# Windowed attention and a low-rank mixer MLP on one core: q and k of eight head pairs transposed by SyncE's transfers, sums that clamp at zero, MLP sums one by one, a new order

## The chip, the cores and the metric

One core of one Trainium2 chip runs the whole program. The metric is device microseconds of one execution; three runs of the kernel before gave 224.15, 224.5 and 225.14 us (median 224.5). PE is TensorE, DVE is VectorE, ACT is ScalarE, POOL is GpSimd, SP is SyncE. [...]

## The reference

```python
# q, k, v: (4, 8, 768, 64); U: (768, 32); V: (32, 768); w_ch1: (512, 2048); w_ch2: (2048, 512); all float32
scores = scale * np.matmul(q, k.transpose(0, 1, 3, 2))
rel = pos[:, None] - pos[None, :]
is_global = pos[None, :] < 8
keep = is_global | ((rel >= 0) & (rel < 96))
dist = np.where(is_global & ~is_local, 96.0, np.abs(rel))
scores = np.where(keep, scores - slopes * dist, -1e9)
a = softmax(scores)
x = (a @ v).transpose(0, 2, 1, 3).reshape(4, 768, 512)
h = x.transpose(0, 2, 1) @ U @ V
u = x + h.transpose(0, 2, 1)
out = u + np.maximum(u @ w_ch1, 0.0) @ w_ch2
```

Of the 768 keys a query sees 8 global ones and the 96 last, so scores are made for a block of 128 queries against its own and the block before it, with the global keys written over 32 rows of the latter.

## The kernel before

**Order.** The kernel is a list of named tasks. Each is made by `add` with an engine, an expected duration, the tasks that it depends on, and the buffers that it takes (`acq`) and gives back (`rel`). `ORDER` names every task once. `Planner.run` goes through that list, gives each task a start by its engine's clock, its inputs and its buffers, and the program is then written in the order of these starts. Every engine works through its own tasks strictly in that order, so the relative order on one engine is the list's, and a task that waits holds up all behind it on its engine. A DMA counts as a task of the engine that issues it: POOL issues the loads (l..., w1_, w2_), SP the stores (O), copies of k and v (KO, VC, VG where CFG says S), and the first pair's loads.

**Attention.** The 4 batches have 8 heads each, two to a pair: pairs 0 to 15, four to a batch. For pair p, lk, lq and lv load k, q and v, cast to 16 bits, into staging buffers (three each for q and k). TK and TQ transpose them on PE by six matmuls with an identity (`flip`, line 608, matmul in line 611; pairs 1 to 3 by twelve of half width, `tr`, line 592) into one PSUM bank, and EK and EQ copy the result on DVE or ACT (`flat`, line 618, through `copy`, lines 362 and 364) into the tiles kT and qT, of which there are three each. KO makes kO, k moved by the global keys (line 653; by DMA through line 366). S makes the scores (line 734), with a bias matmul SB first in pairs 0 to 3; EX takes their exponential on ACT (line 799); MK multiplies by a mask on DVE in pairs 4 to 15 (lines 808, 812); PV multiplies by v and by vo (lines 866, 867); vo is v with the global rows, written by VC and VG. RC and NM divide by the sum (lines 901, 905), XC makes a 16-bit copy of x.

**Mixer.** UP transposes x on PE and multiplies it by U (lines 840, 845), XE and XU turn that small product, TE copies it, HM adds V's product (line 966) and E writes the sum u, transposed, into uT.

**MLP.** The first product has 16 blocks of 128 columns of w1 over 768 tokens. M1a and M1b are plain products (lines 1020, 1044); RL and RM clamp and evict them on ACT into htr (lines 1026, 1062). Pairs of blocks z and z + 8, for z of 4 to 7 in batches 1 and 2 and of 2 to 7 in batch 3, are made by Winograd's variant of Strassen's product: seven products (ZP1 to ZP7, line 1115) in place of eight. For that, ZT makes four sums of u, ZS four sums of w1's blocks (lines 1093 to 1096, kept over the batches for z of 4 to 7), and ZU, ZW, ZX, ZA, ZB, ZD, ZR evict and add the products (`ev`, lines 1133 and 1166). ZA, ZB and ZD are DVE sums of a PSUM bank and a stored product; since they don't clamp, ZQ and ZV clamp htr in place afterwards (lines 1172 and 1174).

The second product is made in the same way over all of w2: PA and PB make the sums of htr (lines 1199 to 1205; two instructions in each task, four pairs of tasks in a batch), TWa and TWb those of w2, RS starts the banks with the mixer's share (line 1238), P1 to P7 are the products (line 1246), DA to DH add them to x (lines 1258, 1285, 1298), O stores.

Where PE would wait in the early stages, the program puts matmuls of zeros (line 1347).

```python
            e1, e2 = ENG[CFG["ZQ"][z]], ENG[CFG["ZR"][z]]
            R1 = ev("Q", e1, ..., flat_relu(e1, htr[:, z]), [C11, C12], fast=1)
            R2 = ev("V", e2, ..., flat_relu(e2, quad(z + hj, 1)), [C22], fast=1)
            relus[z], relus[z + hj] = [R1, C11], [R2, C21]
```

Of the kernel before, what the change touches and what calls it, by code (L numbers as in the profile page):

```python
# [14 lines left out]
ALU = mybir.AluOpType  # L15
# [21 lines left out]
TWb1 S6.1 EX6.1 EX6.2 RS0.1 P10.1 P20.1 DA0.1 mask6 lv6 TQ8 P30.1 DF0.1 TK8 lq10 MK7.0 EQ8 UP5 XE5 VC7 P50.0 lq12
VG7 EK8 XU5 TE5 lk11 mask4 P30.0 DF0.0 S6.0 EX6.0 HM5 E05 MK6.2 P60.0 DB0.0 MK6.1 P60.1 DB0.1 S7.1 MK6.0 EX7.2 RS0.2
MK7.2 P10.2 DA0.2 P70.1 DD0.1 TQ10 lq11 EX7.1 MK7.1 TK9 EK9 KO9 ZS4 P70.0 lv11 TQ9 P20.2 EQ10 VC11 VC6 VG6 EQ9 TK10
EK10 KO10 DD0.0 P40.1 DG0.1 PV7 RC7 NM7 PV6 KO8 RC6 NM6 lv8 P60.2 P30.2 DC0.0 XC7 DB0.2 P50.1 DC0.1 XC6 UP7 UP6 XE7  # L40
DF0.2 P40.0 DG0.0 lv10 XE6 XU6 TE6 XU7 TE7 lv9 P70.2 DD0.2 HM6 E06 HM7 E07 S8.0 EX8.0 lq14 E17 ZP11.5 MK8.0 ZU1.5
# [5 lines left out]
O0.1 NM8 XC8 ZX1.7 PA1.1 S9.0 EX9.0 M1b1.5 M1b1.4 RM1.4 ZP51.6 ZB1.6 ZP41.6 RM1.5 UP8 XE8 MK9.0 ZP51.7 lk12 ZR1.6
TK12 EK12 TD1 ZP31.6 ZB1.7 M1a1.5 ZV1.7 ZD1.6 TQ12 RL1.5 XU8 EQ12 TE8 ZP41.7 ZR1.7 lv12 ZP31.7 ZD1.7 M1a1.0 M1b1.0
HM8 M1a1.1 M1b1.1 MK9.2 ZV1.6 RL1.0 ZQ1.6 ZQ1.7 PA1.3 PB1.1 E08 RL1.1 PA1.0 VG9 PV9 S10.1 RC9 RS1.1 P11.1 P21.1 lv14
P51.1 EX10.2 NM9 S10.0 PB1.3 PB1.0 DA1.1 EX10.1 XC9 S11.0 EX11.0 MK11.0 EX10.0 RS1.0 P21.0 P51.0 DC1.0 S11.1 EX11.2  # L50
P31.0 P11.0 MK10.1 P31.1 UP9 DF1.0 TQ14 VC12 EX11.1 DA1.0 P61.0 XE9 XU9 KO12 EQ14 TE9 MK11.2 MK11.1 VG11 PV11 lk14
TK14 lk15 EK14 DB1.0 P71.0 O1.0 DF1.1 P61.1 lq13 RC11 NM11 MK10.2 DD1.0 XC11 HM9 E09 S12.0 EX12.0 RS1.2 P11.2 P41.0
KO14 S12.1 EX12.1 DB1.1 P71.1 VG12 EX12.2 P31.2 DA1.2 MK10.0 VG10 DD1.1 PV10 MK12.0 TK13 EK13 P61.2 lq15 RC10 TQ13
EQ13 NM10 P21.2 XC10 KO13 UP10 lv13 UP11 XE10 DB1.2 P71.2 XU10 DF1.2 DC1.1 DG1.0 TE10 DD1.2 XE11 XU11 TE11 P41.1
DG1.1 VC14 O1.4 O1.3 HM10 E010 S14.0 EX14.0 HM11 E111 E011 MK12.1 MK14.0 P41.2 ZP12.7 ZU2.7 S14.1 EX14.2 ZT2 MK14.2
EX14.1 M1a2.5 ZP12.6 P51.2 DC1.2 M1a2.1 M1b2.1 TK15 EK15 KO15 ZU2.6 DG1.2 ZP62.6 RL2.5 ZP62.7 ZW2.6 M1b2.4 RL2.1
# [40 lines left out]
class Group:  # L97


    def __init__(self, kind, readers=1, n=1, among=None):  # L100
        self.kind, self.readers, self.n, self.among = kind, readers, n, among
        self.slot, self.since, self.free_at = None, None, 0.0
        self.read = self.written = 0.0


class Planner:


    LANES = 8

    def __init__(self, counts, dma_rate, switch):
        self.tasks, self.names = [], {}
        self.free = {k: [0.0] * n for k, n in counts.items()}
        self.held = []
        self.dma_rate, self.switch = dma_rate, switch

    def add(self, name, *a, **k):
        t = Task(name, *a, **k)
        if t.name in self.names:
            raise ValueError(name)  # L120
        self.names[name] = t
# [1277 lines left out]
```

## Time and profile before

| | |
|---|---|
| three runs | 224.15, 224.5, 225.14 us |
| profiled execution, span | 223.0 us |
| first matmul of the MLP | 28.1 us |
| last matmul starts | 219.5 us |
| matmuls of line 611, PE | 156 |
| filler matmuls (line 1347), busy | 4.2 us, 16 records |
| copies through PSUM into kT and qT by ACT, 768 wide | 17 of 0.81 us |
| granted TensorE clock | 1.000 |
| DMA: by POOL, by SP | 75.6% and 14.2% of 16 engines' span |

How to read it: the span reaches from the first to the last instruction of the profiled execution; the runs are timed around that. In the 40 slices one slice is 5.6 us. The busy time of PE counts the modelled end of each matmul, which overlaps the next one's start; the time from one start to the next is what a matmul takes of PE when it is packed. In a group's row, the first numbers after the bar are the busy time and the mean of one instruction in ns; after the second bar stands the idle time of the engine before the group, with what ended it. In the chain of waits each piece has its start, its length up to the next piece, and its engine and line. For a DMA, the time of the instruction is what SP or POOL needs to issue it, and the landing is counted from there.

### The profile page before, as it was taken

How to read it: one execution, taken by the hardware profiler on the slowest of the kernel's cores; microseconds unless marked ns; L12 is line 12 of the kernel's file. 1: busy time of each engine (PE TensorE's matmuls, PEld its weight loads, DVE VectorE, ACT ScalarE, POOL GpSimd, SP SyncE). 2: the span in 40 equal slices, each digit the busy share in tenths (PEclk: the TensorE clock that was granted, in tenths of full speed). 3: DMA queues.
4: the chain of work that ended last, by engine and by line, in shares of the span. 5: the costliest groups of instructions: out<-in, count | busy, mean ns of one | idle time of the engine just before them, and what ended most of it. 6: DMA issues, size and time to landing. Idle time of an engine off the chain costs nothing.

```text
span 223.0 us, 5965 instructions
## 1 busy us (share of the span) xinstructions
PE 216.4 (97%) x2424; PEld 158.5 (71%) x2424; DVE 181.6 (81%) x403; ACT 147.0 (66%) x260; POOL 73.7 (33%) x97
## 2 busy tenths in 40 slices
PE   8799899999999999999999999999999999999994
PEld 3466656675879976666888876666788875658883
DVE  5688966999987987888978688597978796889872
ACT  7888798768858669788757557787742458782000
POOL 8989959714894940010851000011000000000000
PEclk9999999999999999999999999999999999999999
DMA  6999999999999997662997021409100006000025
GB/s 173 178 170 149 159 161 185 184 206 166 158 157 92 140 191 141 224 46 37 68 116 98 18 79 65 132 4 71 33 0 3 0 3 259 25 1 3 0 97 190
DMA packets 87404, 23.31 MB, mean 104 GB/s; under 512 B 73840, under 2 KB 84784, under 8 KB 87376
## 3 DMA queue, kind: packets, MB, share of 16 engines
q0 software_dynamic: 72880, 13.74, 75.6%
q1 hardware_dynamic: 14496, 9.19, 14.2%
q8 instruction: 19, 0.31, 0.6%
q14 instruction: 9, 0.07, 0.1%
HBM read 27.56 MB, written 6.29 MB: 152 GB/s over the span
## 4 chain that ended last, share of the span: by engine, by line
PE 84%; DMA 7%; POOL 5%; issue 2%; DVE 1%; ACT 0%; DVEq 0%; POOLq 0%
PE ps L1246 34%; PE ps L1115 14%; PE ps L1020 11%; PE ps L1044 7%; PE ps L734 4%; DMA vt<-in_v_dram 4%; PE ps L611 3%; DMA stgq<-in_q_dram 3%; PE ps L840 2%; PE ps L867 2%; PE ps L866 2%; POOL stgq L457 1%; POOL w L507 1%; PE ps L1238 1%; PE ps L966 1%
## 5 line engine op out<-in xcount | busy, mean ns | idle before, releaser
L799 ACT ACTIVATE ep<-ps 128x1024 f16<-128x1024 f32 (+1 forms) x48 | 44.0, 952 | 16.3 <-PE ps L734 15.1
L1246 PEld LDWEIGHTS <-htr 128*128 128x128 f16 x392 | 36.2, 98 | 6.1 <-issue 1.9
L1020 PE MATMUL ps<-uT,w 128*128 128x384 f16 x176 | 33.3, 326 | 0.0
L1258 DVE TENSOR_TENSOR x_sb<-x_sb,ps 128x256 f32<-128x256 f32 (+1 forms) x60 | 26.8, 463 | 7.6 <-PE ps L1246 7.2
L1246 PEld LDWEIGHTS <-sA 128*128 128x128 f16 x288 | 27.4, 98 | 4.2 <-issue 0.7
L461 POOL DMA_DIRECT2D vt<-in_v_dram x16 | 16.7, 1047 | 32.9 <-PE ps L867 29.7
L1026 ACT ACTIVATE htr<-ps 128x384 f16<-128x384 f32 x44 | 20.7, 493 | 5.6 <-PE ps L1020 5.3
L1246 PE MATMUL ps<-w,sA 128*128 128x256 f16 x192 | 24.2, 273 | 0.0
L1246 PE MATMUL ps<-tB,htr 128*128 128x256 f16 (+1 forms) x200 | 24.2, 268 | 0.0
L1020 PEld LDWEIGHTS <-w 128*128 128x128 f16 x176 | 16.5, 98 | 10.6
L1246 PE MATMUL ps<-w,htr 128*128 128x256 f16 x192 | 23.5, 273 | 0.0
L457 POOL DMA_DIRECT2D stgq<-in_q_dram x24 | 19.9, 852 | 5.4 <-PE ps L611 3.3
L1044 PE MATMUL ps<-uT,w 128*128 128x384 f16 x112 | 21.3, 326 | 0.0
L457 POOL DMA_DIRECT2D stgk<-in_k_dram x24 | 20.0, 852 | 2.6 <-DMA w<-in_moe_w_ch_dram 1.0
L1133 DVE TENSOR_TENSOR htr<-ps,zu 128x384 f16<-128x384 f32 x30 | 16.4, 553 | 4.7 <-PE ps L1115 3.0
L362 ACT ACTIVATE zu<-ps 128x384 f32<-128x384 f32 x30 | 14.7, 493 | 5.7 <-PE ps L1115 5.3
L812 DVE TENSOR_TENSOR ep<-ep,mask 128x1024 f16<-128x1024 f16 x24 | 16.2, 684 | 1.4 <-ACT ep L799 0.9
L905 DVE TENSOR_TENSOR x_sb<-ps,rcp 128x768 f32<-128x768 f32 x16 | 15.3, 956 | 0.9 <-DMA vo<-vt 0.4
L1044 PEld LDWEIGHTS <-w 128*128 128x128 f16 x112 | 10.7, 98 | 6.6
L1115 PEld LDWEIGHTS <-w 128*128 128x128 f16 x108 | 10.2, 98 | 6.1
L734 PE MATMUL ps<-qT,kT 64*128 64x128 f16 x192 | 14.0, 217 | 0.4 <-DVE kT L364 0.4
L1115 PE MATMUL ps<-uT,w 128*128 128x384 f16 x56 | 13.4, 326 | 0.0
(124 smaller groups left out, 450.0 us busy)
## 6 DMA issues: line engine op xcount, KB each, us to landing
out_dram<-x_sb SPq DMA_DIRECT2D x20, 256.0 KB, 2.2
vt<-in_v_dram POOLq DMA_DIRECT2D x16, 192.0 KB, 5.9
stgk<-in_k_dram POOLq DMA_DIRECT2D x24, 96.0 KB, 6.6
stgq<-in_q_dram POOLq DMA_DIRECT2D x24, 96.0 KB, 5.6
w<-in_moe_w_ch_dram POOLq DMA_DIRECT2D x8, 256.0 KB, 7.1
w<-in_moe_w_ch_dram POOLq DMA_DIRECT2D x4, 512.0 KB, 11.7
vo<-vt SPq DMA_DIRECT2D x8, 123.8 KB, 2.5
out_dram<-x_sb SPq DMA_DIRECT2D x7, 128.0 KB, 2.2
```

Source lines behind the costliest of these rows:

```text
L457: nc.gpsimd.dma_start(o[:, i], src[b, h0 + i].rearrange("(n p) d -> p n d", p=P))
L461: nc.gpsimd.dma_start(vt[gv.slot][:, :, :, 0:D], v[b, h0:h0 + 2].rearrange("h (n p) d -> p h n d", p=P),)
L734: nc.tensor.matmul(t[:, hi, j * P:(j + 1) * P], lhs, qt[r, i * P:(i + 1) * P], start=not biased, stop=True, skip_group_check=biased,)
L799: nc.scalar.activation(ep[gep.slot][:, :, lo:512], ps[:, gsc.slot:gsc.slot + 2, lo:512], AF.Exp, scale=qk_scale)
L812: nc.vector.tensor_tensor(ev, ev, mv, ALU.mult)
L1020: nc.tensor.matmul(ps[:, g.slot, 0:HS], w1[:, dc, jt * P:(jt + 1) * P], ub[:, dc, i * HS:(i + 1) * HS], start=(dc == 0), stop=(dc == NDC - 1),
L1026: nc.scalar.activation(htr[:, jt, i * HS:(i + 1) * HS], ps[:, g.slot, 0:HS], AF.Relu)
L1044: nc.tensor.matmul(ps[:, g.slot + half, 0:HS], w1[:, dc, jt * P:(jt + 1) * P], ub[:, dc, half * HS:(half + 1) * HS], start=(dc == flat[0]) ...
L1115: nc.tensor.matmul(bank(g), a()[:, i], bq[:, i], start=first and i == 0, stop=last and i == 1, skip_group_check=True,)
L1133: return lambda: nc.vector.tensor_tensor(o, x(), y(), ALU.add)
L1246: nc.tensor.matmul(o if part is None else o[:, part], a[:, j, c0 + cols.start:c0 + cols.stop], bq[:, j] if part is None else bq[:, j, part ...
L1258: nc.vector.tensor_tensor(o, o, x, ALU.add)
```

## The change

What it does:

- For pairs 8 to 15 (`QD`), TK and TQ are gone, and EK and EQ are one transposing DMA each, issued by SP, from the staging buffer into kT or qT.
- ZA, ZB and ZD use one instruction that adds and clamps between 0 and 3e38; ZQ and ZV are gone.
- PA and PB are split into four tasks Sa, Sb, Sc, Sd of one instruction each. P5 now depends on the four Sa, P6 on Sb, P7 on Sc, P3 on Sd.
- The sums of w1's blocks are made for two blocks at a time (ZS1, ZS2, ZS3, 512 columns an instruction) and kept; batch 3's two extra blocks no longer use the buffers of the exponentials. The third set lies over the identity scaled for the bias and an early scratch tile, both of which have served by then.
- Some EK, EQ, KO, TE, XE, XC and E tasks move to another engine.
- The planner counts a small overlap of ACT's and DVE's instructions with the one before, and counts a transposing DMA as 1.0 of SP and 1.0 of transfer.
- `ORDER` is new throughout.
- Options that were not used are deleted, and one (`XD`, empty) is added.

```diff
-    "ZK": (4, 5, 6, 7), ... "ZR": "DDADDAAD", "ZQ": "DDAADDDD", "TE": "DAADAAAADADADAAD", "XE": "DAAAAAADAAAAAAAD",
-    "EK": "ADADDDADAADAAAAD", "EQ": "DDADAADDADADAAAA", "KO": "ADDDDDSDASASSAAD",
-    "XC": "DDDDDQAADADAAAQA", "E": "AAAAAADAADDAAAAA",
+    "ZK": (2, 3, 1),
+    "TE": "ADADAAAAADAAAAAA",
+    "XE": "AAADADAADAAAAAAA",
+    "EK": "ADDDDADDAADAAAAD",
+    "EQ": "DDDADDDDADADAAAA",
+    "KO": "ADDDDDDDASDSDDAS",
+    "XC": "DDDDDQAAADDAAAQD",
+    "E": "AAAAAADAAAAAADAA",
+    "TSP": 1.0,
+    "TSZ": 1.0,
+    "XD": (),
+    "NZS": 2,
+    "QD": (8, 9, 10, 11, 12, 13, 14, 15),
...
+    OVER = {ACT: 0.105, DVE: 0.08}
...
         def arrange(x, stg, gs, ld, gt, dst, i):
+            if p in CFG["QD"]:
+                def turn():
+                    o = dst().rearrange("c (n p) -> c n p", n=NB)
+                    nc.sync.dma_start_transpose(o, stg[gs.slot].rearrange("p a b -> p (a b)"))
+
+                return [add(SP, TSP, turn, ld, acq=[gt], rel=[gs], size=TSZ, name=f"E{x}{p}")]
             g = Group("ps", among=A1)
...
+                def sums_s(home=home, A11=A11, A12=A12, A21=A21, A22=A22):
+                    op = nc.vector.tensor_tensor
+                    op(home[:, 1], A11, A21, ALU.subtract)
+                    op(A21, A21, A22, ALU.add)
+                    op(home[:, 0], A21, A11, ALU.subtract)
+                    op(home[:, 2], A12, home[:, 0], ALU.subtract)
...
             def tt(o, x, y):
-                return lambda: nc.vector.tensor_tensor(o, x(), y(), ALU.add)
+                return lambda: nc.vector._custom_dve(TENSOR_ADD_SAT, out=o, in0=x(), in1=y(), s0=3.0e38, s1=0.0)
...
-            R1 = ev("Q", e1, {ACT: 0.84, DVE: 0.4, POOL: 2.2}[e1], flat_relu(e1, htr[:, z]), [C11, C12], fast=1)
-            R2 = ev("V", e2, {ACT: 0.47, DVE: 0.26, POOL: 1.16}[e2], flat_relu(e2, quad(z + hj, 1)), [C22], fast=1)
-            relus[z], relus[z + hj] = [R1, C11], [R2, C21]
+            relus[z], relus[z + hj] = [C11, C12], [C22, C21]
...
-            p1 = add(ea, 0.57 if by_dma else 1.14, pre1, need, fast=2 if by_dma else 12, name=f"PA{b}.{g}")
-            p2 = add(eb, 1.02 if eb == DVE else 4.6, pre2, [p1] + war(3), fast=12, name=f"PB{b}.{g}")
-            pa += [p1, p2]
+            def one(nm, o, x, y, op, dp):
+                return add(DVE, 0.555, lambda: nc.vector.tensor_tensor(o, x, y, op), dp, fast=2, name=f"{nm}{b}.{g}")
+
+            T1 = one("Sa", s1, a21, a22, ALU.add, need + war(5))
+            T3 = one("Sc", a21, a11, a21, ALU.subtract, [T1])
+            T2 = one("Sb", s2, s1, a11, ALU.subtract, [T1] + war(6))
+            T4 = one("Sd", s4, a12, s2, ALU.subtract, [T2] + war(3))
```

The parts of the two lists that the prediction speaks of; first around the start of the MLP, before and after:

```diff
-VG3 EX2.0 E00 SB3.2 w1_7 S3.2 w1_6 PV2 RC2 NM2 UP1 XC2 EX3.0 TQ4 EX3.2 lk7 PV3.0 PV3.1 PV3.2 RC3.2 XE1 XU1 RC3.0
-M1a0.3 M1c0.3 HM3 E03 vs2 E13 KO5 S4.1 lv4 EX4.1 mask0 EX4.2 M1d0.3 M1b0.3 RL0.3 M1a0.14 M1b0.14 w1_4 RL0.14 M1b0.15
-lq6 M1b0.13 RM0.13 M1a0.2 M1c0.2 TK7 M1d0.2 MK4.1 RM0.15 w1_2 MK4.2 VC4 M1a0.13 VG4 RM0.14 EK7 KO7 RL0.13 M1b0.2
+TK5 XU2 E01 TE2 UP3.0 UP3.1 HM2 EK5 UP3.2 EQ4 S4.0 NM3 XE3 E02 XU3 TE3 KO5 S4.1 HM3 EX4.0 w1_0 E03 E13 M1a0.1 lq5
+M1c0.1 w1_3 M1d0.1 M1b0.1 lk6 w1_2 mixl TK6 EX4.1 RL0.1 M1b0.6 EX4.2 M1a0.5 TQ5 M1b0.7 M1a0.6 RL0.5 RM0.6 mask0 EK6
+EQ5 KO6 TD0 RM0.7 S5.1 MK4.2 RL0.6 MK4.0 lk7 w1_5 vs2 lv4 EX5.2 MK5.2 VC4 lv5 w1_7 S5.0 EX5.0 M1a0.11 M1b0.4 lq6 EX5.1
```

and in the new list around the last transposing DMAs:

```diff
+DC1.1 lq13 lv12 VC12 DD1.1 DD1.2 lv14 lk13 UP11 XE11 EQ14 P41.2 XE10 XU11 XU10 DF1.0 TE11 DB1.0 P71.0 DG1.2 VG12 TE10
+S14.0 HM11 HM10 E111 E010 DD1.0 E011 ZT2 P41.1 EX14.0 ZP12.6 P41.0 ZP22.6 M1a2.0 ZP12.7 ZU2.6 M1b2.0 ZP62.6 DG1.1
...
+ZU2.5 ZB2.6 ZP12.4 ZP22.5 ZP62.7 ZW2.7 M1a2.6 ZA2.5 MK12.1 ZP42.6 ZP32.6 ZP62.5 ZA2.7 O1.5 EK15 VG15 VC15 VC14 O1.2
+O1.3 O1.1 EQ13 ZU2.4 EQ15 M1b2.6 ZP22.4 RL2.6 ZW2.5 ZD2.6 ZP72.7 ZR2.6 ZA2.4 RM2.6 ZX2.7 ZP62.4 ZW2.4 S14.1 ZP52.7
...
+MK14.0 O1.4 MK14.2 Sa2.3 MK14.1 PV12 ZP52.5 KO15 RM2.4 ZP42.5 RC12 ZR2.4 NM12 PV14 RL2.2 ZR2.5 S13.0 EX13.0 RC14 ZB2.5
```

More of the change, by code (lines that the diff above doesn't have):

```diff
@@ L37 @@
[L37 to L41, printed above, removed]
@@ L47 @@
[L47 to L51, printed above, removed]
@@ L52 @@
[L52 to L56, printed above, removed]
@@ new lines @@
+lv8 lq10 M1b0.13 M1b0.11 TWa1 TWb1 PV6 M1a0.14 RM0.13 UP5 M1a0.13 RL0.14 RM0.11 RC6 NM6 Sa0.1 RL0.15 XE5 RL0.13
+M1b0.14 S7.0 RS0.2 XU5 P10.2 VG7 VC7 VC8 RM0.14 RS0.0 VG8 EQ8 EK9 EK8 EQ9 KO9 Sa0.2 Sb0.2 Sc0.2 EX7.0 Sb0.1 MK7.2
+DA0.2 TWa0 RS0.1 lv10 TE5 lk12 Sa0.3 Sb0.3 HM5 Sd0.2 Sd0.3 MK7.1 P20.0 lv9 P20.1 lq11 lk15 E05 P10.0 XC6 UP6 P50.1
+P10.1 Sd0.1 XE6 XU6 TE6 Sc0.3 TWb0 P50.2 HM6 E06 DA0.1 DA0.0 P30.1 P20.2 P30.0 MK7.0 Sc0.1 P60.1 P60.2 DC0.1 DB0.1 PV7
+RC7 P60.0 P50.0 NM7 P70.1 DF0.0 DC0.0 XC7 UP7 XE7 DB0.2 DB0.0 DD0.1 DF0.1 P30.2 DF0.2 XU7 P70.0 TE7 HM7 E17 E07 DD0.0
@@ L186, in run @@
             s = max(r, clock[t.eng])
+            if t.eng in self.OVER and t.eng in last:
+                p = last[t.eng]
+                s = max(r, p.start + 0.02, clock[t.eng] + (0.035 if p in t.deps else -self.OVER[t.eng]))
+                if p in t.deps:
+                    s = max(s, p.end + 0.035)
+            last[t.eng] = t
             if t.eng == PE and t.mode != mode:
@@ L342 @@
     zu = sb("zu", [P, HS], FP32, CFG["NZU"])
-    zs = sb("zs", [P, len(ZK), 3, 2, P], FP16) if ZK else None
+    NZS = CFG["NZS"]
+    zs = sb("zs", [P, NZS, 3, 2, 2 * P], FP16)
+    zh = [zs[:, i] for i in range(NZS)] + [ibe[:, 0:12 * P].rearrange("p (i a c) -> p i a c", i=3, a=2)]
     assert hj == H and HS == 384
@@ L934, in attention @@
             XC = add(
-                xe, 0.9 if xq else {DVE: 0.55, POOL: 0.88, ACT: 0.84}[xe], cast, [NM], acq=[gx16], size=1.2 if xq else 0.0, fast=1, name=f"XC{p}",
+                xe, 0.9 if xq else {DVE: 0.6, POOL: 0.88, ACT: 0.84}[xe], cast, [NM], acq=[gx16], size=1.2 if xq else 0.0, fast=1, name=f"XC{p}",
             )
+            gx16.readers = 1 + turned
             UP = add(
-                PE, 0.49 if xu else 0.67, mixed(range(NB)), [XC, c_u16], lat=0.3, acq=[gx], rel=[gx16],
+                PE, 0.16 if turned else 0.49, mixed(range(NB)), [XC, c_u16], lat=0.3, acq=[gx], rel=[gx16],
@@ new lines, in attention, with xturn, xuevac @@
+            if turned:
+                def xturn():
+                    o = uT[b % 2][:, hp].rearrange("p (n c) -> p n c", n=NB)
+                    nc.sync.dma_start_transpose(o, x16[gx16.slot].rearrange("p n c -> p (n c)"))
+                XT = [
+                    add(
+                        SP, TSP, xturn, [XC] + (mm1_done[b - 2] if b >= 2 else []), size=TSZ, rel=[gx16], name=f"XT{p}",
+                    )
+                ]
+        gxu = Group("xu")
+        def xuevac():
+            copy(ENG[CFG["XE"][p]], xus[gxu.slot], ps[:, gx.slot, 384:384 + R].unsqueeze(1).broadcast_to((P, RG, R)))
@@ L956, in tevac, with xuturn @@
+        def xuturn():
+            nc.tensor.matmul(
+                ps[:, gx.slot + 1, 384:512], xus[gxu.slot].rearrange("p g r -> p (g r)"), ident16,
+                start=turned, stop=True, skip_group_check=True,
+            )
+        XE = add(ENG[CFG["XE"][p]], 0.28, xuevac, [UP], acq=[gxu], name=f"XE{p}")
+        UP = add(PE, 0.06, xuturn, [XE], lat=0.3, rel=[gxu], name=f"XU{p}")
+        if split:
+            assert not turned
+            XT = []
         def tevac():
-            copy(ENG[CFG["TE"][p]], tmp[b % 2][:, hp * P:(hp + 1) * P], ps[:, gx.slot + int(xu), 384:512])
+            copy(ENG[CFG["TE"][p]], tmp[b % 2][:, hp * P:(hp + 1) * P], ps[:, gx.slot + 1, 384:512])
@@ L1110, in bank, with pr @@
                 return ps[:, g.slot, 0:HS]
-            def pr(n, g, a, bq, dp, reads=False, first=False, last=False, z=z, gs=gs):
+            def pr(n, g, a, bq, dp, reads=False, first=False, last=False, z=z):
                 def go():
@@ L1119, in pr @@
                 t = add(
-                    PE, 0.327, go, dp, lat=0.3, acq=[g] if first else [], bw=[] if first else [g],
-                    rel=[gs] if reads and gs else [], name=f"ZP{n}{b}.{z}",
+                    PE, 0.327, go, dp, lat=0.3, acq=[g] if first else [], bw=[] if first else [g], name=f"ZP{n}{b}.{z}",
                 )
@@ L1300, in mlp @@
             DC = add(DVE, 0.7, both, [P5], rel=[gX], name=f"DC{b}.{t}")
-            if acc:
-                def onto(gst=gst, t=t):
-                    nc.gpsimd.dma_start(xb[:, t + ht], late[gst.slot], accum_op=ALU.add)
-                DG = add(POOL, 1.0, onto, [DD, DG, DC], rel=[gst], size=0.9, name=f"AX{b}.{t}")
             def store(tt, c0, c1):
```

292 lines of the change are left out of this document (126 added, 166 removed).

## The prediction

> **What bounds the kernel now.** I read the page first (busy shares, then the 40 slices), then the chain of waits in order of time, then the groups by line, then the SP queue's own issues.
>
> ```profile
> span 223.0 us, 5965 instructions
> ...
> PE 216.4 (97%) x2424; PEld 158.5 (71%) x2424; DVE 181.6 (81%) x403; ACT 147.0 (66%) x260; POOL 73.7 (33%) x97
> ...
> PE   8799899999999999999999999999999999999994
> ```
>
> PE is the bound, and from the eighth slice (39 us) to the last but one it has no hole. A busy PE can still hide waits, because a matmul's end is modelled: the groups give 0.22 us for one transpose, while starts lie much closer. So the price of PE work is taken from the chain, where a piece lasts until the next one starts:
>
> ```profile
> 60.02 0.34 PE ps L611 x6
> 60.36 0.87 PE ps L1246 x8
> 61.23 0.33 PE ps L611 x6
> ```
>
> Six transposes of one q or k hold PE for 0.34 us, 0.057 us each, with no pause before or behind. The transposes are thus on the path, at that price. Before 39 us the chain is another one: loads, and engines that wait for them.
>
> ```profile
> 26.86 8.09 DMA vt<-in_v_dram
> ...
> 34.97 0.77 DVE vo L364
> ...
> 36.01 0.55 DVE kT L364
> ...
> 36.60 0.34 PE ps L734 x6
> ```
>
> Here the copy of v for pair 4 (VC4) stood at the head of DVE's queue until its load landed at 34.95; the k of a later pair was written behind it, and PE's scores started at 36.60.
>
> **The change part by part.**
>
> *Transposes off PE.* For pairs 8 to 15, TK and TQ go: 16 tasks of 6 matmuls, 16 x 0.34 = 5.4 us of PE, all of it after 58 us, where PE is packed. Nothing replaces it on PE. This is the main term: -5.4. Adding up the PE tasks of the two order lists at prices from such rows gives 204.7 before and 199.3 after, so no other PE work changes. Stretches of row-grouped matmuls (scores, mixing, rest) between full ones are 35 before and 38 after by my count in the lists; a change of kind costs PE some 0.1 us (an estimate: sixteen scores hold 0.55 us, but the six of 36.60 hold 0.34 with the change behind them). I take +0.3, bounds 0 to 0.6.
>
> *Their evictions.* Sixteen PSUM copies go too: 12 on ACT (0.81 each, 9.7 us) and 4 on DVE (0.56, 2.2 us). Worth nothing on the path: neither engine ends a wait of PE there (the only compute engine that PE itself is seen waiting for after the first microseconds is DVE, 0.4 us, at 36.6).
>
> *The transfers that replace them.* SP gets 16 issues that the trace of before doesn't show. The nearest rows are SP's other SBUF-to-SBUF transfers:
>
> ```profile
> L366 SPq DMA_DIRECT2D vo<-vt x24: 585/616/2116, 62.1 to 156.5; - x24
> ...
> L366 SPq DMA_DIRECT2D kO<-kT x8: 612/650/1747, 46.2 to 102.7; - x8
> ...
> DMA to landing us min/median/max: 1.9/2.4/9.2
> ```
>
> Between 0.6 and 2.1 us to issue, 1.9 to 9.2 us to landing for 120 KB; these move 192 KB. I take 1.0 us of SP and 4 us to landing (kO's median is 3.9), since size and kind are kO's. That is 16 us of SP over 90 us, in a queue with holes of up to 27 us. Does any come too late? By PE work counted along the new list, EK8, EQ8, EK9 and EQ9 stand 17 us ahead of the first score that reads them (S9.0), EK10 and EQ10 7 us (S10.1), EK14 17 us, but EQ14 only 2.0 us before S14.0 and EK13 2.2 us before S13.0. A place in the list is no time: SP runs ahead where it is free. Ahead of EK13, SP holds EK15, the copies of v for 15 and 14, four stores, EQ13 and EQ15; the first can start when the second MLP's sums end, 19 us of PE work before S13.0. Four transfers at t, nine plain issues at about 0.5 and 4 us to landing and copy: 4t + 8.5, so 12.5 at t = 1.0, and no wait below t = 2.6. EQ14 waits for its load (lq14, 16 us of PE work ahead; loads land in 3.6 to 14.5) and then 4 us. I charge +0.4 for small waits at S14.0 and S13.0; bounds 0 (landing in time) and 4 (2 us at each). Behind a transfer that waits on SP stand stores and copies of v; PV waits for the copies, and a store's buffer is next written two batches on, which is far.
>
> [...]
>
> *Sums that clamp.* 42 sums (ZA, ZB, ZD) clamp at zero, and ZQ and ZV go.
>
> ```profile
> L1133 DVE TENSOR_TENSOR htr<-ps,zu 128x384 f16<-128x384 f32 x30 | 16.4, 553 | 4.7 <-PE ps L1115 3.0
> ...
> L1174 DVE TENSOR_SCALAR htr<-htr 128x768 f16<-128x768 f16 x12 | 4.1, 355 | 0.2
> ...
> 183.00:201.30 18.30, 18.30 (x123) 11.06 (x121) 15.00 (x34) 14.71 (x33) 0.00 (x0) 1.00 0.23 87
> ```
>
> Gone: 12 x 0.355 and 7 x 0.255 = 6.0 us of DVE, 5.2 us of ACT. The new sum isn't in the trace; same operands and count as the old, so I take 0.55; it can hardly be below the 0.355 of a clamp alone, and 1.1 (a second pass) is the other end. At 0.55 the path gains nothing, since PE covers it. The cover is thinnest in the last MLP's first product, 183 to 201.3: DVE 15.0 of 18.3, of which its 18 sums are 9.9. It loses 2.2 in clamps there; at 1.1 the sums add 9.9, 22.7 in 18.3: 4.4 us late.
>
> *The rest.* Weight sums: 24 instructions of 0.28 become 12 of about 0.42 (between 0.28 for 256 columns and 0.55 for 768), -1.7 us of DVE. PA and PB become four tasks each of the same instructions: 64 x 0.55, unchanged, free to lie apart. Moves between engines (EK and EQ of pairs 0 to 7, KO, TE, XC, E) add about 2.6 us to DVE. DVE ends near 174 of 181.6, ACT near 129 of 147. All of it lies under PE.
>
> *New order, start.* Until its first MLP matmul at 28.1 us, PE has 4.2 us of filler matmuls and some waits, one of 0.5 at 36.60 shown above. In the new list VC4 comes after the first scores of pair 5, and lv4 after the loads of k for pairs 5 to 7, so that block goes: -0.5. Other loads move by one or two places of about 0.85 us on POOL; bounds -3 (most filler gone) to +2.
>
> Sum: 223.0 - 5.4 + 0.3 + 0.4 - 0.5 = 217.8 us of span. The runs' median is 224.5, 1.5 over the profiled span, so **219.3 us**.
>
> **The rivals.**
> - *The start gains more.* Speaks for it: ACT and DVE are both near 80% busy before 30 us, and six evictions there change engines. Against: real PE work ahead of the first MLP matmul is the same 17 to 18 us in both lists, and the loads' time isn't changed. 3 us more: 216.3.
> - *Waits at S14.0 and S13.0 take much of it.* Loads of 14 land late and each score waits 2 us: 219.3 + 3.6 = 222.9, with no difference if another microsecond follows.
> - *Slower: the transposes fill SP.* If one holds SP or its rings for t, the stretch EK15 to EK13 is 4t + 8.5 against 19 us. Waits begin at t = 2.6, the gain is gone at t = 4.0, and t = 5.3 gives 219.3 + 4 x 2.7 = 230; at the 9.2 us of the longest landing, 245. For it: kO's landing varies fourfold. Against: no SP issue in the trace passes 2.1 us.
> - *The clamped sum costs 1.1:* the last stage comes 4.4 us late, 223.7; no change.
>
> **How the numbers follow.** The forecast 0.61, own range 217 to 221.5; better start 0.15; waits at two scores 0.09; costly sum 0.04; slower 0.11. A measurement of this kernel can't tell 0.5% (1.1 us) from no change. Faster (under 223.4): 0.61 + 0.15 + most of the waits = 0.84; same 0.05; slower 0.11. The range 215 to 224.5 leaves out the slower case and a small part below.
>
> **What would show it.** Right: no L611 rows of pairs 8 to 15, PE's matmuls fewer by 96, PE without holes from 40 us, SP's transposes under 2.6 us each, L1174 and L1172 gone with the sums still near 0.55. Wrong: PE idle at scores of pairs 8 to 15 with a DMA into qT or kT as releaser; sums near 1 us; a first MLP matmul later than 30 us.

## Result and the profile after

| | before | after |
|---|---|---|
| median of four runs beside each other | 224.56 us | 232.29 us (230.72 to 232.99) |
| ratio, 95% interval | | 1.0333 [1.0292, 1.0374] |
| span of the profiled execution | 223.0 us | 231.2 us |
| mean granted TensorE clock | 1.000 | 0.976 |

The kernel became 3.3% slower; the forecast was 219.3 us. Some executions of a kernel take over 1.5% longer than its fastest, and all times and ratios here leave those out. Every ratio below is against the kernel before, run beside it (medians 224.5 to 225.1 us). The page of the kernel after, its head and the 40 slices (one slice is 5.8 us):

```profile
span 231.2 us, 5730 instructions
...
PE 216.4 (94%) x2330; PEld 154.9 (67%) x2330; DVE 172.9 (75%) x374; ACT 129.1 (56%) x235; POOL 74.0 (32%) x97
...
PE   8999997999999389999976999999999999999994
...
PEclk9999999999999959999997999999999999999999
DMA  7999999999994993999499957851300001000346
```

PE now has two holes, in slices 14 and 15 (75 to 87 us) and in slices 21 and 22 (116 to 127 us), and at each the clock digit falls, to 5 and to 7. The last row is one that the prediction didn't read: no slice of the DMA engines is under 0.9 from 6 to some 70 us. In the kernel before this stretch reaches to 84 us:

```profile
DMA  6999999999999997662997021409100006000025
```

The row adds up the times of all packets and is cut off at 9. The times of packets that overlap count together, so the share of a window can pass 1 (2.30 from 80 to 85 us, below); a stretch of 0.9 or more is called full here.

To see where time goes I price all PE work at its packed start-to-start times from the trace: 205.2 us before, 199.9 us after. At a moment, that moment plus the work still to do is the earliest end still open. Where a column grows from one row to the next, that time was lost (e1, e2, e3 and e6 are experiments, described below):

| at | before | after | e1 | e2 | e3 | e6 |
|---|---|---|---|---|---|---|
| 28 us | 214.4 | 207.6 | 208.0 | 207.8 | 208.1 | 207.3 |
| 75 us | 216.2 | 211.5 | 210.8 | 211.6 | 211.4 | 211.6 |
| 90 us | 216.7 | 219.5 | 212.8 | 217.2 | 213.8 | 212.7 |
| 110 us | 217.1 | 220.0 | 213.6 | 217.9 | 214.7 | 213.7 |
| 130 us | 217.8 | 226.0 | 219.4 | 220.2 | 216.4 | 214.4 |
| last matmul | 219.5 | 227.8 | 221.1 | 222.0 | 218.1 | 216.0 |

At 75 us the kernel after is 4.7 us ahead. It loses 8.0 us between 75 and 90 and 6.0 between 110 and 130 (before: 0.5 and 0.7). The chain of waits of the kernel after shows the first hole (start, length, engine and line; L652 is the transposing transfer, L408 SP's copies, L767 the scores, L1263 the second product):

```profile
75.97 0.56 SPq L652
...
76.63 0.69 SPq L408
...
77.38 4.28 DMA kO<-kT
...
81.79 0.40 PE ps L767 x4
82.19 5.17 PE ps L1263 x24
```

S9.0 waits for q of pair 9, and then for kO9, the last thing that SP issued. The 24 matmuls behind take 5.17 us; at the packed 0.109 us they are 2.6. Why SP is late stands in its own timeline of the kernel after (start, us, instruction):

```profile
68.26 1.91 SPq L408 DMA_DIRECT2D vo<-vt  x3
70.28 2.08 SPq L652 DMA_TRANSPOSE qT<-stgq  x1
72.55 2.61 SPq L652 DMA_TRANSPOSE kT<-stgk  x2
75.32 1.21 SPq L652 DMA_TRANSPOSE qT<-stgq  x1
76.63 1.39 SPq L408 DMA_DIRECT2D kO<-kT  x2
```

and in SP's waits of that stretch:

```profile
SPq L408 <- DMA vt<-in_v_dram: 19.6, 1, 19.6
```

VC8, the copy of v for pair 8, stands ahead of EQ8 in SP's list and waited until v8 had landed at 68.2. The four transfers and KO9 came in one row behind it. The second hole, by the chain (L832 is the exponential, L404 ACT's copy that makes KO14):

```profile
116.38 5.21 DMA kT<-stgk
...
121.62 0.83 ACT kO L404 x2
122.45 0.92 ACT ep L832
...
125.79 3.01 PE ps L1263 x16
```

EK14 was issued at 116.4 and landed at 121.6. KO14 waited for it on ACT, in front of the exponential of pair 11, for which PV11 waited on PE. And SP came late to EK14 because KO11, also on SP, had waited for the landing of EK11:

```profile
SPq L408 <- DMA kT<-stgk: 5.1, 1, 5.1
```

The clock of both holes, by windows of the kernel after (PE, PEld, DVE, ACT and POOL busy, then the granted clock, DMA share, GB/s):

```profile
75.00:80.00 5.00, 2.12 (x20) 1.42 (x17) 2.44 (x6) 0.90 (x3) 4.16 (x5) 1.00 1.18 140
80.00:85.00 5.00, 3.21 (x18) 2.23 (x19) 0.69 (x1) 1.53 (x3) 3.42 (x5) 0.53 2.30 151
85.00:90.00 5.00, 5.00 (x49) 3.48 (x48) 1.65 (x5) 2.32 (x3) 0.00 (x0) 0.78 0.29 21
90.00:95.00 5.00, 5.00 (x45) 2.99 (x43) 4.86 (x11) 4.37 (x7) 0.00 (x0) 1.00 0.87 265
```

So of the 8.0 us some 5 are the waits themselves and 2.6 the slower clock behind them. The 0.53 and 0.78 are means of windows of 5 us: in shorter windows the trace has 0.50 from 80.3 to 87.2 us and 1.00 around it, and behind the second hole 0.50 from 124.7 to 128.1 us.

The transfers and the clamped sums themselves, by line of the kernel after (issue time in ns min/median/max):

```profile
L652 SPq DMA_TRANSPOSE qT<-stgq x8: 1210/1253/2085, 70.3 to 148.0; - x8
L652 SPq DMA_TRANSPOSE kT<-stgk x8: 1212/1245/2033, 72.6 to 150.7; - x8
...
  POOL stgk L499: 22.8, 3
...
DMA to landing us min/median/max: 2.7/3.6/6.4
```

```profile
L1182 DVE CUSTOM_DVE_ANT_0 htr<-ps,zu 128x384 f16<-128x384 f32 x30 | 16.3, 553 | 12.4 <-PE ps L1165 7.9
```

At the median a transfer costs SP 1.25 us and lands 3.6 us after its issue, both near the 1.0 and 4 of the forecast (EK11 and EK14, of the second hole, took 6.4 and 5.2), and the clamped sum takes the 553 ns of the plain one. POOL waited 22.8 us in all for k's staging buffers to be given back.

### The profile page after: what moved, and what is told of

It reads as the page before. It is cut to its first block, busy times and chain, and to the rows that moved or that the text cites. A ratio compares the mean times of both kernels' runs of the same rounds, so it can differ in the third digit from the quotient of the medians.

```text
span 231.2 us, 5730 instructions
## 1 busy us (share of the span) xinstructions
PE 216.4 (94%) x2330; PEld 154.9 (67%) x2330; DVE 172.9 (75%) x374; ACT 129.1 (56%) x235; POOL 74.0 (32%) x97
## 4 chain that ended last, share of the span: by engine, by line
PE 78%; DMA 10%; DVE 4%; POOL 3%; ACT 2%; issue 1%; SPq 1%; DVEq 0%; ACTq 0%; POOLq 0%
PE ps L1263 31%; PE ps L1165 14%; PE ps L1071 8%; PE ps L1095 7%; PE ps L767 4%; DMA stgq<-in_q_dram 4%; PE ps L895 2%; DMA kT<-stgk 2%; DMA x<-x_sb 2%; PE ps L874 2%; PE ps L748 2%; DMA kO<-kT 2%; PE ps L894 2%; PE ps L1255 1%; PE ps L1350 1%; PE ps L1009 1%
## 5 line engine op out<-in xcount | busy, mean ns | idle before, releaser
L832 ACT ACTIVATE ep<-ps 128x1024 f16<-128x1024 f32 (+1 forms) x48 | 44.3, 953 | 16.9 <-PE ps L767 16.4
L1263 PEld LDWEIGHTS <-htr 128*128 128x128 f16 x392 | 37.7, 101 | 7.4 <-issue 2.1
L1071 PE MATMUL ps<-uT,w 128*128 128x384 f16 x176 | 33.9, 326 | 0.1
L1263 PEld LDWEIGHTS <-sA 128*128 128x128 f16 x288 | 27.8, 100 | 4.6 <-issue 0.8
L499 POOL DMA_DIRECT2D stgk<-in_k_dram x24 | 19.9, 844 | 24.3 <-DMA kT<-stgk 22.8
L1263 PE MATMUL ps<-tB,htr 128*128 128x256 f16 (+1 forms) x200 | 26.0, 286 | 0.0
L1182 DVE CUSTOM_DVE_ANT_0 htr<-ps,zu 128x384 f16<-128x384 f32 x30 | 16.3, 553 | 12.4 <-PE ps L1165 7.9
L1263 PE MATMUL ps<-w,sA 128*128 128x256 f16 x192 | 24.7, 274 | 0.0
L1077 ACT ACTIVATE htr<-ps 128x384 f16<-128x384 f32 x44 | 20.6, 493 | 6.4 <-PE ps L1071 6.2
L1263 PE MATMUL ps<-w,htr 128*128 128x256 f16 x192 | 23.8, 273 | 0.0
L1071 PEld LDWEIGHTS <-w 128*128 128x128 f16 x176 | 16.2, 98 | 10.5 <-DMA w<-in_moe_w_ch_dram 0.5
L1095 PE MATMUL ps<-uT,w 128*128 128x384 f16 x112 | 21.3, 326 | 0.0
L404 ACT ACTIVATE zu<-ps 128x384 f32<-128x384 f32 x30 | 14.2, 495 | 6.9 <-PE ps L1165 6.6
L767 PE MATMUL ps<-qT,kT 64*128 64x128 f16 x192 | 14.6, 220 | 2.0 <-DMA qT<-stgq 2.0
L895 PE MATMUL ps<-vt,ep 128*128 128x65 f16 x192 | 13.3, 193 | 3.2 <-ACT ep L832 3.2
L895 PEld LDWEIGHTS <-ep 128*128 128x128 f16 x192 | 12.5, 97 | 4.7 <-issue 3.4
L1095 PEld LDWEIGHTS <-w 128*128 128x128 f16 x112 | 10.6, 98 | 7.1 <-issue 0.3
```

Source lines behind the costliest of these rows:

```text
L499: nc.gpsimd.dma_start(o[:, i], src[b, h0 + i].rearrange("(n p) d -> p n d", p=P))
L767: nc.tensor.matmul(t[:, hi, j * P:(j + 1) * P], lhs, qt[r, i * P:(i + 1) * P], start=not biased, stop=True, skip_group_check=biased,)
L832: nc.scalar.activation(ep[gep.slot][:, :, lo:512], ps[:, gsc.slot:gsc.slot + 2, lo:512], AF.Exp, scale=qk_scale)
L895: nc.tensor.matmul(o, e[:, hi, (j + 1) * P:(j + 2) * P], vv[:, hi, i, 0:D1], start=(i == 0), stop=True)
L1071: nc.tensor.matmul(ps[:, g.slot, 0:HS], w1[:, dc, jt * P:(jt + 1) * P], ub[:, dc, i * HS:(i + 1) * HS], start=(dc == 0), stop=(dc == NDC - 1),
L1077: nc.scalar.activation(htr[:, jt, i * HS:(i + 1) * HS], ps[:, g.slot, 0:HS], AF.Relu)
```

## Experiments

**Theory Q:** the transfers are cheap, and what costs is SP's queue, in which they stand behind tasks that wait for a landing. **Rival T, later B:** the transfers cost by themselves, through the DMA engines.

**e1, e2, e3: two places in the list.** e1 moves five tasks of SP ahead of VC8; e2 moves one task of ACT; e3 does both.

```diff
-VG7 VC7 VC8 RM0.14 RS0.0 VG8 EQ8 EK9 EK8 EQ9 KO9 Sa0.2
+VG7 VC7 EQ8 EK9 EK8 EQ9 KO9 VC8 RM0.14 RS0.0 VG8 Sa0.2
...
-lv11 KO14 VG11 EX11.1 P51.2 VC11 EX11.2
+lv11 VG11 EX11.1 P51.2 VC11 EX11.2
...
-EX12.1 UP8 PV11
+EX12.1 KO14 UP8 PV11
```

> The changed kernel with one move on SP: the transposes of pairs 8 and 9 and KO9 stand ahead of VC8 and VG8, not behind. Theory Q (the time is lost because SP's queue stands behind the landing of v8, and scores 9 then wait): the hole of PE at 76 to 82 us (2.3 + 2.9 us) goes and with it the low granted clock after it (2.6 us); 232.3 - 7.7 = about 224.6, the hole at 120 to 124 stays. Rival T (a transposing DMA is slow in itself, wherever it stands): S9.0 still waits, less than 2 us gained. Rival O (the new order of PE is bad): no gain.

> The changed kernel with one move on ACT: KO14, which reads a transposed k, stands behind the exponentials of pairs 11 and 12, not ahead of them. Theory Q: the hole of PE at 120 to 124 us (3.4 us) goes, and the low clock after it (1.5 us); about 227.5, the hole at 76 to 82 stays. Rival T: k14 lands late all the same and PE waits at another place, under 2 us gained. Rival O: no gain.

> Both moves together. Theory Q: the two holes and the low clock behind them are 8.0 + 5.3 us of lag against the kernel before, so 232.3 - 13 = 219 to 220, faster than the kernel before by 2%, near the 219.3 that was forecast. Rivals T and O: above 226.

Measured: e1 225.06 us, ratio 1.002 [0.998, 1.006]; e2 227.46 us, 1.011 [1.007, 1.015]; e3 222.70 us, 0.990 [0.984, 0.995]. Each move removes most of its own hole and leaves most of the other: by the table e1 loses 2.0 us from 75 to 90 and 5.8 from 110 to 130 us, e2 5.6 and 2.3, the kernel after 8.0 and 6.0. PE's waits in e1 from 60 to 130 us are

```profile
PE ps L895 <- ACT ep L832: 3.8, 1, 3.8
PE ps L767 <- DMA kO<-kT: 1.3, 1, 1.3
```

So 9.6 us between the kernel after and e3 hang on where six tasks stand; nothing was computed differently. Q holds for the two big holes. But e3 is some 3 us over its expectation, and PE still waits 1.6 us for kO9 and 1.0 us for v11's copy. In e1 the transfers were issued at 60.9 to 67.6 us, 8 to 9 us earlier than in the kernel after, and took 6.4 to 7.8 us to land in place of 2.7 to 3.6: earlier in the list means deeper in the stretch where the DMA engines are full (in the kernel after their share is 2.44 and 1.69 in the two windows from 60 to 70 us, and 0.49 from 70 to 75). That this is what e3 lacks is not shown yet; it is where B comes in.

**e4: the clamping sums alone,** in the old order, with the sixteen transposes on PE; ZQ and ZV issue nothing.

```diff
-                return lambda: nc.vector.tensor_tensor(o, x(), y(), ALU.add)
+                return lambda: nc.vector._custom_dve(TENSOR_ADD_SAT, out=o, in0=x(), in1=y(), s0=3.0e38, s1=0.0)
```

> The kernel before, its order and plan kept, with the clamping sums and without the 28 instructions of ZQ and ZV. Theory: a clamping sum costs the same 0.55 us, and what goes lies under PE; within 0.5% of before (223.5 to 225.7), DVE busy 6 us less. Rival: DVE's relief closes waits of PE in the MLP stages, 1 to 2 us faster.

224.65 us, ratio 0.9993 [0.997, 1.002]: no part of the result. VectorE is busy 176.8 us in place of 181.6, 4.8 less where 6 were expected.

**e8: KO11 off SP.** In the kernel after, KO11 alone goes to VectorE (`"KO"`, place 11: S to D, and later in the list).

> The kernel after with one change: the copy of keys with offset of pair 11 (KO11) goes from SP to VectorE, so that SP doesn't wait 5 us for the landing of pair 11's k before it issues EQ11, EQ12 and EK14. If the second loss (5.3 us at 120 to 130) comes from this wait in SP's queue, most of it goes: 227 to 228 us. If EK14 is late for another reason (lk14's landing, a full kT buffer) or KO11 makes VectorE wait instead, little goes: 231 to 232.3 us.

226.88 us, ratio 1.009 [1.005, 1.012]. The second loss is gone by another way than in e2, which leaves KO11 alone: between 110 and 130 us the earliest end grows by 1.1 us in place of 6.0. EK14 is issued at 107.7 us in place of 116.4, while PE itself is only some 1.5 us earlier there. KO11's wait on SP was the cause of EK14's lateness.

**e5: the transfers alone, in the old order,** for six pairs.

```diff
         def arrange(x, stg, gs, ld, gt, dst, i):
+            if p in (8, 9, 12, 13, 14, 15):
+                def turn():
+                    o = dst().rearrange("c (n p) -> c n p", n=NB)
+                    nc.sync.dma_start_transpose(o, stg[gs.slot].rearrange("p a b -> p (a b)"))
+
+                return [add(SP, 1.0, turn, ld, acq=[gt], rel=[gs], size=1.0, name=f"E{x}{p}")]
             g = Group("ps", among=A1)
```

> The kernel before, with its own order, its clamping copies and its joint loops, in which q and k of six pairs (8, 9, 12, 13, 14, 15) are turned by SyncE's transposing transfers: 12 of the 16 transposes of the change, and nothing else of it; each transfer stands in SP's list where the copy out of PSUM stood or at the transpose's place. Theory Q (a transposing transfer is cheap; what cost the time after was what stood ahead of and behind the transfers in SP's list): 12 x 0.34 = 4.1 us of TensorE leave, small waits stay, 220.5 to 222.5 us against 224.6. Rival T (the transposing transfers cost the time by themselves, by their bandwidth, by staging buffers that they hold longer, or by TensorE's clock): 12/16 of the 13 us lost in the kernel after less 4.1, some 228 to 230 us.

232.84 us, ratio 1.036 [1.030, 1.042]. This is slower than even the rival's 228 to 230, and it showed that Q was not all. PE waited 5.1 us at 72 us for the load of q10, which took 10.9 us to land (5.7 in the kernel before) with three transfers under way beside it, two issued before it and one 1.9 us after, and 2.2 us at 123 us for v11's copy.

**e9, e10: transfers that nobody reads,** on top of the whole kernel before, four in the full stretch or eight in the quieter one behind it (DMA share of the kernel before 1.70 and 1.94 from 40 to 60 and 60 to 80 us, then 0.95, 0.89 and 0.32 in the next three stretches of 20 us; within the 0.89 the window from 110 to 115 us has 2.02, above the 0.0 to 0.7 that e10's expectation goes by).

```diff
+            if p in (8, 9):
+                def extra(d=dum[nd[0] % 2]):
+                    nc.sync.dma_start_transpose(d.rearrange("c (n p) -> c n p", n=NB), w1.rearrange("p a b -> p (a b)")[:, 0:S])
+
+                nd[0] += 1
+                add(SP, 1.0, extra, ld, size=1.0, name=f"Y{x}{p}")
```

> The kernel before, whole, with four transposing transfers on top that nobody reads: at the places in SP's list where pairs 8 and 9 are turned in the kernel of the six pairs (57 to 75 us), each after its pair's load has landed, 128x768 in 16 bits, from a part of w1 into buffers that are idle by then. They hold no staging buffer, and TensorE still turns q and k itself. The 16 DMA engines are full there (9 in every slice up to 60 us). Theory B (each such transfer takes some 1.6 us of all DMA engines, so the loads behind them land later: q of pair 10 by 4 to 5 us): TensorE waits 2 to 4 us for q10 and runs at a lower clock after it, 228 to 231 us. Theory H (what cost the time was staging buffers and places held behind a landing, not the transfer): 224.6 to 225.5 us.

> The same with eight such transfers at the places of pairs 12 to 15 (about 95 to 135 us), where the DMA engines are busy for 0.0 to 0.7 of the time. Theory B: there is room, so 224.6 to 225.5 us. If a transposing transfer disturbs TensorE or the other transfers wherever it runs: 8/4 of what the four early ones cost, 230 us or more.

e9 228.07 us, ratio 1.016 [1.013, 1.018]; e10 224.64 us, 1.002 [1.000, 1.005]. Four early ones cost 3.5 us, eight late ones nothing that can be told. e9's waits of PE from 55 to 80 us, and the landing of its four transfers:

```profile
PE ps L612 <- DMA stgq<-in_q_dram: 2.7, 2, 1.5
```

```profile
DMA to landing us min/median/max: 8.1/9.8/10.6
```

e10's landing, and its SP queue in the page's list of DMA queues (packets, MB, share of 16 engines; 14.2% before):

```profile
DMA to landing us min/median/max: 2.8/3.8/4.5
```

```profile
q1 hardware_dynamic: 20896, 10.76, 19.6%
```

19.6% of 222.6 us is 43.6 us of all sixteen engines, before it was 14.2% of 223.0, 31.7. Eight transfers took 12.0 us more, 1.5 each, for 0.196 MB each. This adds up the packets' times, overlaps included, and the same reckoning for e9's four (18.7% of 226.4 us) gives 2.7 each. So 1.5 is an estimate from above of what one takes of the engines. In the full stretch it is taken from loads: six loads of q take 6.5 to 7.3 us to land in e9 (issued from 60.8 us on), the same six 4.7 to 5.7 in the kernel before; over all eight that are issued from 55 to 75 us the medians are 6.7 and 5.0. B holds: q's loads come late although no staging buffer is held and POOL's list is the old one.

**e13, e14, e15: e5 taken apart.** Pairs 8 and 9 alone; pairs 12 to 15 alone; the latter with one task moved:

```diff
-EQ14 VC12 EX11.1 DA1.0 P61.0 XE9 XU9 KO12 TE9 MK11.2 MK11.1 VG11 PV11
+VG11 EQ14 VC12 EX11.1 DA1.0 P61.0 XE9 XU9 KO12 TE9 MK11.2 MK11.1 PV11
```

> The kernel before, its own order, with q and k of pairs 8 and 9 alone turned by SyncE's transfers (4 transposes, 1.36 us, leave TensorE). Theory B (the DMA engines are full up to 75 us): the 3.5 us that four such transfers cost there when nobody read them, less 1.4, plus what TensorE's shorter list adds to its wait for q10: 226.5 to 229 us. If the transfers that are needed cost no more than they save: 223.2 to 224.6 us.

> The kernel before, its own order, with q and k of pairs 12 to 15 alone turned by SyncE's transfers (8 transposes, 2.72 us, leave TensorE). Theory B with the order of SP's list: room on the DMA engines, so up to 2.7 us are gained; the kernel of the six pairs waited 2.3 us there for v11's copy, which stands on SP behind pair 14's q and pair 12's keys with offset, so 222 to 224.6 us. If late transfers lose too once the kernel depends on them: 225 to 228 us.

> The same with one task moved: v11's second copy (VG11) ahead of pair 14's q (EQ14) in SP's list. Theory B with the order of SP's list: the wait for v11 goes or halves, 221.8 to 222.8 us, faster than before by 0.8 to 1.2%. If SP's list is not what makes v11 late (its load lands late): as without the move.

e13 230.62 us, ratio 1.026 [1.021, 1.032]; e14 226.34 us, 1.007 [1.004, 1.010]; e15 223.26 us, 0.992 [0.989, 0.995]. e13 is over its range: PE, freed of 1.4 us of transposes just ahead of it, waits the longer for q10 (5.1 us, against 2.7 us in e9's two waits together); the load lands at 73.0 us (71.6 in e9), and the clock is 0.50 for 3.4 us behind the wait. Work taken off PE ahead of a wait for a load was no gain. POOL also waited 3.9 us for a staging buffer that a transfer held, which e9 leaves out; its share in what e13 loses beyond e9 was not measured apart. e14 fell into the range that was written for late transfers losing too. e15, 0.5 us over its range but inside it as a ratio, says why they do: not by themselves, but by one place in SP's list. The chain of waits in e14:

```profile
110.22 1.07 SPq L623
...
111.39 0.66 SPq L364
...
112.09 0.72 SPq L364
...
112.86 1.03 SPq L364
...
113.93 5.89 DMA vo<-vt
```

EQ14 (L623) first waits 8.0 us at the head of SP's queue until PE's scores free its buffer. Then come the two parts of KO12, then VG11: SP takes another 3.9 us before v11's copy is on its way, and the copy lands 5.9 us later. By then POOL's eight loads of k and q (107.6 to 113.2 us) are under way; ahead of them, at 101 us, such a copy landed in 1.9 us. With VG11 ahead of EQ14, PE has no wait over 0.2 us from 105 to 130 us. One task in a list of some 1,100 is worth 1.5% here (1.007 against 0.992).

**e6 and e11: towards a better kernel.** e6 is e3 with KO9 and KO11 on VectorE, v11 loaded and copied earlier, q5 loaded earlier. e11 is e6 with pair 5's cast of x (XC5) moved from POOL's transfers to VectorE and q5's load put between its two places.

> The kernel after with both moves, and further: the copies of keys with offset of pairs 9 and 11 (KO9, KO11), which stand on SP behind the landing of their own transposing transfer, are made by VectorE; v11 is loaded and copied earlier; q5 is loaded earlier. Theory Q: the waits of 1.8 us (S9.0, for KO9's copy), 1.1 us (PV11, for v11) and 1.1 us (q5's transpose) go, so 222.7 less 3 to 4: 218.7 to 219.7 us, faster than before by 2.2 to 2.6%. Rival (each wait that is taken away shows the next one just behind it, so that the order has no lead left): 221.5 to 222.7 us.

> The kernel with the copies of keys off SP, with two changes: the cast of x for pair 5, a transfer of POOL that took 9 us to land in the full stretch, is made by VectorE, and q5's load stands three POOL transfers later than in that kernel (earlier than in the kernel after). The wait of 1.44 us at 56 us (transpose of x5) goes and the 1.12 us at 29 us shrinks: 221.7 less 1.4 to 2.5, 219.2 to 220.3 us. If loads just land later by as much (the DMA engines are the bound up to 60 us): 221 to 222 us.

e6 221.68 us, ratio 0.987 [0.982, 0.992], the fastest of all and faster than both kernels, but only 1.0 of the 3 to 4 us that were expected beyond e3, with intervals that overlap. The three waits are gone, but with q5's load earlier other transfers came later, and PE waited 1.0 us at 29 us (k5) and 1.3 us at 56 us (x5). e11 222.71 us, 0.994 [0.991, 0.998]: not better. Its profile ends at the same 216 us of the table. The rival in both expectations is nearer than theory Q. That the DMA engines are the bound up to 60 us, so that a load moved ahead moves others back, fits both runs; no run tests it apart.

**e7, e12: what lowers the clock.** Products of zeros in PE's waits of the kernel after, 92 and 60 in e7, 78 in the first alone in e12.

```diff
+            if t.name == "S9.0":
+                idle(78, P, [g for g in t.acq if g.kind == "ps"][0].slot)
```

> The kernel after, with products of zeros in TensorE's two long waits: 92 products of 128x128 (0.056 us each, 5.1 us) right ahead of S9.0's score product and 60 (3.3 us) right ahead of PV11, into the bank that the next task writes anyway. If the granted clock of 0.53 to 0.8 after the two waits comes from TensorE having stood idle, the clock stays near 1.0 there and 2.5 + 1.3 us come back: about 228.5 us. If the clock falls for another reason (the work after them, the engines that run at once), nothing comes back: 232.3 us, or some more where the products of zeros overrun the wait.

> The kernel after with 78 products of zeros (4.4 us) right ahead of S9.0 and none elsewhere: in the kernel with both waits filled, the second group ran after its wait was over (at 130 us) and cost 3.3 us by itself, while the clock of 80 to 90 us stayed at 1.0. If the low clock after the first wait comes from TensorE standing idle: 232.3 less 2 to 2.5, 229.8 to 230.3 us. If not: 232.3 us or more.

e7 234.74 us, ratio 1.043 [1.035, 1.050]; e12 233.58 us, 1.036 [1.031, 1.041]. The clock stayed up where PE was kept busy, 1.00 in both in place of 0.53 and 0.78; the same two windows in e12:

```profile
80.00:85.00 5.00, 5.00 (x76) 4.63 (x74) 0.48 (x1) 1.46 (x3) 3.40 (x5) 1.00 2.28 147
85.00:90.00 5.00, 5.00 (x68) 3.62 (x66) 3.00 (x8) 3.45 (x6) 0.00 (x0) 1.00 0.34 45
```

and its earliest end grows from 75 to 90 us by 5.3 us in place of 8.0. But the time didn't come back. In e12's profile PE waited 1.4 us for x5 at 57 us, where the kernels are the same (0.3 in the kernel after), and the second hole came as before; in e7 the second group of zeros ran after its wait. That the clock fell with PE idle in this hole and not with the hole filled is shown; that filling it is worth 2 us is not.

## Why the prediction was wrong

The gain on PE came as forecast. The step that failed is the price of the transfers that pay for it.

- **Transposes off PE, -5.4: right.** PE's work fell by 5.3 us. The +0.3 for changes of kind was not measured apart.
- **Evictions, sums, weight sums, moves: right.** DVE was forecast near 174 and is 172.9, ACT near 129 and is 129.1; the clamped sum is 0.553 us; e4 moved nothing.
- **The transfers, "+0.4 for small waits at S14.0 and S13.0; bounds 0 and 4": this step failed.** The two losses are 14.0 us, 12.8 over what the kernel before loses there, and neither is at S14.0 or S13.0. Three things in it were wrong.
  1. *Lead was counted in PE work.* "EK8, EQ8, EK9 and EQ9 stand 17 us ahead" is true of PE's list, and the text said itself that a place is no time, but only the stretch from EK15 to EK13 was followed on SP. On SP, VC8 held EQ8 until 68.2, and KO11 waited 5.1 us in front of EK14. The kernel's own planner does put VC8 in front, but by its durations VC8 starts at 64.0 and S9.0 has its inputs in time.
  2. *The lead was counted to the wrong reader.* EK14 stands 17 us ahead of S14.0, but its first reader is KO14, on ACT, with pair 11's exponential behind it. In the first hole too the last to come was kO9, made by SP from pair 9's k after its landing, and not a transfer of EQ or EK itself.
  3. *The DMA engines were taken as free.* The 4 us to landing came from kO's median. A transfer took 1.5 us of all sixteen engines' packet time in e10, and where they are full that is taken from loads (in e9 q's land in 6.7 us at the median, in the kernel before in 5.0). The row that the prediction used showed it: its 9.2 us is a kO of 40 KB at 47 us, while the two kO at 102 us landed in 2.2 and 2.5 us. (The row isn't one of 120 KB alone, as the text has it; it also holds copies of 20.6 and 40 KB.)
- **The slower rival** put its price into SP's time for one issue, t. That was 1.25 and would have made no wait; 230 us at t = 5.3 is near the result by accident. A wait in front of the transfers and full DMA engines weren't among the rivals.
- **The start, -0.5:** after 28 us the kernel after is 1.5 us better than the transposes explain; by 75 us 0.6 worse, mostly from a wait of 1.5 us for q5 at 39 us.
- **A wait's price:** counted as its length. The first hole, 4.7 us of waits, cost another 2.6 us in clock, about half as much again.

## What to carry to other kernels

In this kernel, work that moves to a DMA queue has three prices: the issue (1.25 us at the median), the place behind everything in that queue that waits for a landing (VC8's wait of 19.6 us, KO11's of 5.1), and the share of the DMA engines; read the DMA row of the page first, since eight such transfers from 93 us on cost nothing that can be told (e10) and four between 48 and 75 us cost 0.9 us each (e9). Count lead time on the queue that issues and to the first instruction that reads, on whichever engine that is, not on the engine that is the bound. A task that waits for a landing belongs behind the transfers that others need, or on an engine that has time to wait.

## What the hardware showed that I had not expected

In the kernel after the granted clock was 0.50 from 80.3 to 87.2 us and from 124.7 to 128.1 us, 6.8 and 3.4 us, and 1.00 around them. It fell within the second of two waits, 2.0 and 2.7 us with two matmuls between them, and held for 6.8 us; in e13, behind a wait of 5.1 us, it was 0.83 in the two windows from 70 to 80 us, which is 3.4 us at 0.50. e3, whose longest wait of PE is 1.6 us, has a mean of 1.000, and where products of zeros filled the first hole it stayed at 1.00 (e7, e12). The length of a wait doesn't decide alone in these runs: e14, with one of 2.2 us, has a mean of 0.999, and e5, with one of about that length at 123 us, has 0.85 and 0.81 in the two windows from 120 to 130 us. And a transfer landed later where the DMA engines carried more. In the kernel after, the one issued at 73.9 us landed in 2.7 us, with a DMA share of 0.74 over that time, the one at 104.3 in 6.4 with 1.44 and the one at 116.4 in 5.2 with 1.55. In e9, where the share is 1.61 from 40 to 60 us and 2.35 from 60 to 80, the four took 8.1 to 10.6 us, and SP's time to issue one lay between 1.2 and 3.7 us.
